# One 128-row load of the last V block, issued as three loads of 112, 8 and 8 rows

## The chip, the cores and the metric

The kernel runs on one core of one Trainium2 chip. The metric is device time in microseconds (us), as the median of several executions; besides these there is one profiled execution, from which every line of the profile comes. The core has a matrix engine (PE in the profile; PEld is its weight load), a vector engine (DVE), a scalar engine (ACT), GpSimd (POOL) and SyncE (SP), which in this kernel does nothing but issue transfers. The transfers themselves are carried out by the core's 16 DMA engines.

## The reference, cut to what matters

All arrays are float32. One token goes through four blocks: attention, MLP, attention, MLP, both attention blocks with the same caches and weights, and so both MLPs.

```python
def _A_ref(x, k_cache, v_cache, wq, wo):          # 32 heads, 4096 keys, 128 per head
    q = (x @ wq).reshape(B, Sq, H, Dh).transpose(0, 2, 1, 3)
    scores = jnp.einsum("bhqd,bhkd->bhqk", q, k_cache) * (Dh ** -0.5)
    p = _softmax(scores, axis=-1)
    o = jnp.einsum("bhqk,bhkd->bhqd", p, v_cache)
    return o.transpose(0, 2, 1, 3).reshape(B, Sq, H * Dh) @ wo

def _B_ref(x, w1, b1, w2, b2):                     # 512 -> 1376 -> 512
    return _gelu(x @ w1 + b1) @ w2 + b2

x = A_x
x = x + _A_ref(_layernorm(x), A_k_cache, A_v_cache, A_wq, A_wo)
x = x + _B_ref(_layernorm(x), B_w1, B_b1, B_w2, B_b2)
x = x + _A_ref(_layernorm(x), A_k_cache, A_v_cache, A_wq, A_wo)
x = x + _B_ref(_layernorm(x), B_w1, B_b1, B_w2, B_b2)
```

K and V hold 64 MB each and are needed in both layers, so that some 285 MB are read in all.

## The kernel before, in words

The 32 heads are worked in eight groups of four heads. K and V of a group are each one block of 128 rows (partitions) by 16384 columns, 8 MB. A block is cut into eight chunks of 2048 columns, numbered 0 to 7; a chunk is one step of the scores (K) or of the values (V) on PE. The first layer takes the groups upwards, the second downwards, so that what is still in SBUF at the change of layers is used again.

SBUF holds one large array, `arena`; every load goes to a place of it that is worked out by hand. All loads but one small one of vectors are issued by SP, through the helper `load` (L108 to L111 of the kernel before), each as one transfer of 128 rows, and they stay in the order in which the program calls `load`. A load waits until the place that it overwrites has been read. A load also signals its end on one of eight semaphores that the loads use in turn (DMAHW0 to DMAHW7 below), and it is not issued before the load that used the same semaphore last, eight loads earlier, has landed. So up to eight loads are issued and not yet landed, and the DMA engines work through them in the order of issue.

In a group, PE makes the scores from K, DVE and ACT make the exponentials, and the values are made partly by PE (`values`) and partly by DVE (`weighted`, `added`). The last group of the second layer is worked otherwise, from L579 on: its V block comes in four loads, which the table `LAST = ((0, 4), (4, 6), (6, 7), (7, 8))` gives as first and last chunk, and `values` multiplies each chunk on PE as soon as it has come. Behind these four loads SP issues the output weights of the group (one load of 2048 columns), the first MLP weights (2752, 1376 and 1376 columns) and the second MLP weights (2048, 2048, 1024 and 512 columns). These eight loads are the last of the program. `head_out`, `set_x` and `mlp` use them in that order, and the result, 2 KB, is written by SP at the end.

The generator `blocks` (L386) is what loads a block piece by piece and hands its chunks to the loop. The change touches `load`, `blocks` and the loop at L579.

Of the kernel before, what the change touches and what calls it, by code (L numbers as in the profile page):

```python
# [17 lines left out]
P = 128  # L18
# [5 lines left out]
C = 8  # L24
# [5 lines left out]
NC = 4 * U  # L30
# [24 lines left out]
W1_AT_END = ((0, 2), (2, 3), (3, 4))  # L55
LAST = ((0, 4), (4, 6), (6, 7), (7, 8))
W2_AT_CHANGE = (0, W1C, 2 * W1C, 3 * W1C, 10 * U, 11 * U)
W2_AT_END = (0, 4 * U, 8 * U, 10 * U, 11 * U)


@with_exitstack
def decode_layers(ctx: ExitStack, tc: tile.TileContext, vectors, k, v, w, w1, w2, out):
    nc = tc.nc
# [41 lines left out]
    def at(first, n):  # L105
        return arena[:, first : first + n]

    def load(first, src):  # L108
        t = at(first, src.shape[-1])
        tc.keep_in_program_order(nc.sync.dma_start(t, src))  # L110
        return t  # L111

    def matmul(*a, **kw):
# [5 lines left out]
    def quarters(first):  # L119
        return [at(first + U * j, U) for j in range(4)]  # L120

    def part(src, g, a, b):
        return src[g][:, NC * a : NC * b]

    def of_w(row, i, n):
        return w[row][:, NC * i : NC * (i + n)]

    def by_four(t):
        return t.rearrange("p (j n) -> p j n", j=4)


    wq_t = by_four(load(SHARED, of_w(1, 0, 1)))
    nc.vector.memset(wide, 1.0)
    nc.vector.memset(cells[:, WIDE:], 0.0)
# [52 lines left out]
    def set_x(xin0, scale, xin1, queries=True):  # L187
        s = small("x_sum")
        t = x_wide if queries else small("x1", 8)
        if not queries:  # L190
            nc.gpsimd.memset(pairs(t)[:, :, 1], 1.0)
        x = pairs(t)[:, :, 0]
        nc.vector.scalar_tensor_tensor(x, xin0, scale, xin1, op0=ALU.mult, op1=ALU.add, accum_out=s)
        if queries:
            for j in range(1, J):
                nc.gpsimd.tensor_copy(pairs(t[:, 32 * j :])[:, :, 0], x)
        return t, s

    def idle(to, n=U, of=C_AT, amid=False):
        matmul(to[:, :n], zero[:, 0:1].to_broadcast([P, P]), at(of, n), start=not amid, stop=not amid)  # L200
# [71 lines left out]
    def values(i, pt, vt, c):  # L272
        for j in range(J):
            matmul(pO[32 * j : 32 * j + 4, :], pt[:, c, j, :], vt[j],
                   start=(i == 0), stop=(i == C - 1))
# [11 lines left out]
    def added(home, by_pe=BY_PE):  # L287
        first, n = home + NC * by_pe, C - by_pe
        while n > 1:
            m = n // 2  # L290
            a, b = at(first + NC * (n - 2 * m), NC * m), at(first + NC * (n - m), NC * m)
            pinned(a, a, b, op=ALU.add)
            n -= m
        return quarters(first)
# [19 lines left out]
    def head_out(rl, wt, last=False, home=None, clear=0):  # L314
        on = head(rl, last)
        if clear:
            idle(pO[:, U - clear :], clear)
        to = pS if last else pO
        out_product(on, wt, to, last)
        return of_32(turned(to, not last, home), 4)  # L320
# [56 lines left out]
    def load_w1(first, a, b):  # L377
        load(first + W1C * a, w1[:, W1C * a : W1C * b])

    def load_w2(first, a, b):  # L380
        load(first + a, w2[:, a:b])

    def in_rows(first, n, rows):
        return [at(first + n * i, n) for i in range(rows)]

    def blocks(src, g, home, pieces=((0, C),)):  # L386
        for a, b in pieces:
            load(home + NC * a, part(src, g, a, b))
            for c in range(a, b):
                yield c, quarters(home + NC * c)  # L390

# [20 lines left out]
    def next_queries(xs, negm, wt, to=pO):  # L412
        for c in range(4):
            wide_query_block(to, c, xs, wt)
        z = queries(to, negm, wide=True)
        if to is pS:
            nc.vector.memset(pS, 0.0)
        return z
# [7 lines left out]
    def group(z, acc, ahead, k_blocks, out_behind=C - 2, change_banks=False):  # L426
        nonlocal pS, pO, pT, pM
        for c, t in k_blocks:
            scores(z, c, t)
            if ahead and c == SUM_BEHIND:  # L430
                t, rl, wt = ahead
                sum_up(t)
                on = head(rl)
            if ahead and c == out_behind:
                out_product(on, wt, pO)
        p = exponentials(sc, nsc)
        if ahead:
            acc = add_up(acc, of_32(turned(pO, wide=True), 4))
        if change_banks:
            pS, pO = pO, pS  # L440
            pT, pM = in_blocks(pO), pS
        return acc, *weights(p)

    def partly(pt, v_blocks, home, by_pe=BY_PE):
        for c, t in v_blocks:
            if c < by_pe:
                values(c, pt, t, c)
        weighted(pt, home, by_pe)
# [6 lines left out]
    for g in range(G):  # L455
        final = g == G - 1
        k_home, v_home = RING[2 * g % 3], RING[(2 * g + 1) % 3]
        acc, pt, rl = group(z, acc, ahead, blocks(k, g, k_home, HALVES if final else ((0, C),)))
        ahead = None
        if g == G - 2:  # L460
# [3 lines left out]
        if g < G - 2:  # L464
            partly(pt, blocks(v, g, v_home), v_home)
            pair = load(PAIR, of_w(g % 2, g, 2))
            z = next_queries(xs, negm, by_four(pair[:, NC:]), to=pS)
            ahead = added(v_home), rl, by_four(pair[:, :NC])
            continue
        for c, t in blocks(v, g, v_home, LAST if final else ((0, C),)):  # L470
            values(c, pt, t, c)
            if final and c in (5, 6):
                matmul(pO[:4, :], zero[:, 0:1].to_broadcast([P, 4]), at(C_AT, U), start=False, stop=False)
            if final and c == 7:
                idle_aside(3)
            if g == G - 2:
                for j in range(J):
                    i = 4 * c + j - KEPT_V // U
                    if i >= 0:
                        if pK[i] is pM:  # L480
                            nc.scalar.copy(tail, t[j][:, ASIDE:])
                            nc.scalar.copy(pM[:, :ASIDE], t[j][:, :ASIDE])
                        else:
                            nc.scalar.copy(pK[i], t[j])
# [21 lines left out]
    def behind_w2(c):  # L506
# [7 lines left out]
        if c == 9:  # L514
            begin_k(SHARED + 2 * NC, 2)

    own, xb = mlp(x1, s1, in_rows(SHARED, W1C, 4), in_rows(SHARED, U, FB),
                  lambda i: load_w2(SHARED, *W2_AT_CHANGE[i : i + 2]), behind_w2)
    xs, s = set_x(own, 1.0, xb)
    g = G - 2  # L520
# [30 lines left out]
    for i, first in enumerate([SHARED, SHARED + U] + [PAIR + U * j for j in range(4)]):  # L551
        t = at(first, U)
# [14 lines left out]
    for n in range(2, G):  # L567
        g, final = G - 1 - n, n == G - 1
        k_home, v_home = homes[(2 * n - 1) % 3], homes[2 * n % 3]
        acc, pt, rl = group(z, acc, ahead, blocks(k, g, k_home, HALVES if final else ((0, C),)),  # L570
                            C - 1 if final else C - 2, change_banks=final)
        if not final:
            by_pe = BY_PE_AT_BEGIN if n == 2 else BY_PE
            partly(pt, blocks(v, g, v_home, ((0, 6), (6, 8)) if n == 2 else ((0, C),)), v_home, by_pe)
            pair = load(PAIR, of_w(g % 2, g - 1, 2))
            z = next_queries(xs, negm, by_four(pair[:, :NC]), to=pS)
            ahead = added(v_home, by_pe), rl, by_four(pair[:, NC:])
            continue
        for c, t in blocks(v, g, v_home, LAST):  # L579
            values(c, pt, t, c)  # L580
            if c in (5, 7):
                idle(pS)
        wo_t = by_four(load(PAIR, of_w(g % 2, g, 1)))
        for a, b in W1_AT_END:
            load_w1(A_AT, a, b)
        for a, b in zip(W2_AT_END, W2_AT_END[1:]):
            load_w2(A_AT + 11 * U, a, b)
        own = head_out(rl, wo_t, last=True)
        idle(pO)
# [46 lines left out]
```

## Time and profile before

| | |
|---|---|
| median of 3 executions | 671.42 us (671.38 to 671.7) |
| profiled execution, its own time | 671.53 us |
| its span, first to last instruction | 669.8 us |
| mean granted TensorE clock | 0.804 |
| busy: PE, DVE, ACT | 57%, 56%, 4% of the span |
| DMA: mean rate, share of the last chain of work | 427 GB/s, 62% |
| HBM read | 285.35 MB |

The page of the profile gives the busy time of each engine, a strip of the span in 40 slices, the DMA queues (q1 is the queue of SP's loads), the chain of work that ended last, the costliest groups of instructions and the DMA issues. Views of the trace cut out stretches: busy time by windows, where the column before the last is the mean busy share of the 16 DMA engines and the last is what they moved in GB/s; the chain of waits in order of time; the instructions in order of time; and for the transfers of one tensor, the time from issue to landing. Times within the trace count from the span's start.

### The profile page before, as it was taken

To read this page: it belongs to the slowest core of one execution; us is meant where nothing else is said; L and a number is where in the kernel's file an instruction comes from. 1 tells how busy PE (TensorE), PEld (TensorE's weight loads), DVE (VectorE), ACT (ScalarE), POOL (GpSimd) and SP (SyncE) were. 2 spreads that over 40 slices of the span, in tenths; PEclk is the share of its full clock that TensorE was granted. 3 is DMA by queue.
4 is the path that set the end of the run, shared out by engine and by line. 5 is a ranking of instruction groups with operands and counts; after the bars stand their busy time and mean duration, and the time that the engine had idled before them with its cause. 6 is when DMAs were issued, how large, how long until landed. Compare 5 with 4: busy or idle time off the path is not lost.

```text
span 669.8 us, 5573 instructions
## 1 busy us (share of the span) xinstructions
PE 382.2 (57%) x2356; PEld 109.6 (16%) x2356; DVE 372.5 (56%) x474; ACT 29.7 (4%) x59; POOL 4.9 (1%) x23
## 2 busy tenths in 40 slices
PE   3441742636618446276778978627516456186686
PEld 1010110101101101011214222102101111021122
DVE  2049478395693965942212221492893966938831
ACT  0010000000000000002011120000000000000010
POOL 1000000000000000000000000000000000000000
PEclk9567875876778858787979999977859767786699
DMA  9999999999999999999999999999999999999996
GB/s 384 431 438 439 435 438 438 403 467 432 438 431 410 436 434 440 438 431 416 433 418 408 432 448 424 442 435 435 434 438 401 457 439 438 427 432 411 434 420 275
DMA packets 11544, 285.70 MB, mean 427 GB/s; under 512 B 1536, under 2 KB 1536, under 8 KB 3968
## 3 DMA queue, kind: packets, MB, share of 16 engines
q1 hardware_dynamic: 11376, 285.35, 99.0%
q8 instruction: 18, 0.29, 0.2%
q14 instruction: 6, 0.05, 0.0%
q10 hardware_dynamic: 144, 0.01, 0.0%
HBM read 285.35 MB, written 0.00 MB: 426 GB/s over the span
## 4 chain that ended last, share of the span: by engine, by line
DMA 62%; PE 28%; DVE 5%; another core or an unknown queue 2%; issue 1%; SPq 1%; ACT 0%; POOL 0%; DVEq 0%; ACTq 0%
DMA arena<-in_k 32%; DMA arena<-in_v 20%; PE pO L114 14%; PE pS L114 13%; DMA arena<-in_w 9%; DVE arena L280 3%; SPq L110 1%; DMA front<-in_vectors 1%; DVE arena L180 0%; ACT arena L117 0%; DVE arena L302 0%; PE pS L260 0%; DVE arena L184 0%; DVE cells L246 0%
## 5 line engine op out<-in xcount | busy, mean ns | idle before, releaser
L280 DVE TENSOR_TENSOR arena<-arena 128x2048 f32<-128x2048 f32 (+4 forms) x44 | 260.7, 5924 | 18.1 <-DMA arena<-in_v 17.3
L114 PE MATMUL pS<-arena,front 128*8 128x512 f32 (+2 forms) x466 | 72.6, 728 | 103.9 <-DMA arena<-in_k 103.9
L114 PE MATMUL pO<-arena,front 128*8 128x512 f32 (+3 forms) x602 | 86.1, 672 | 74.3 <-DMA arena<-in_k 49.0
L114 PE MATMUL pO<-arena,cells 128*128 128x512 f32 (+4 forms) x384 | 79.5, 462 | 21.6 <-DMA arena<-in_w 8.0
L114 PE MATMUL pS<-arena,cells 128*1 128x128 f32 (+3 forms) x320 | 58.4, 429 | 12.7 <-DMA arena<-in_w 9.7
L114 PE MATMUL pO<-arena 128*4 128x512 f32 x288 | 48.5, 806 | 19.9 <-DMA arena<-in_v 18.2
L302 DVE STREAM_TRANSPOSE arena<-pO 128x512 f32<-128x512 f32 x9 | 6.5, 717 | 63.6 <-PE pO L114 63.6
L114 PEld LDWEIGHTS pO<-arena,front 128*8 128x8 f32 (+1 forms) x602 | 19.3, 101 | 134.8 <-DVE arena L280 64.3
L114 PEld LDWEIGHTS pS<-arena,front 128*8 128x8 f32 (+1 forms) x466 | 15.0, 106 | 159.2 <-DVE arena L280 96.9
L180 DVE STREAM_TRANSPOSE arena<-pO 32x128 f32<-32x128 f32 x60 | 18.7, 312 | 39.3 <-PE pO L114 38.1
L114 PEld LDWEIGHTS pO<-arena,cells 128*128 128x128 f32 (+3 forms) x384 | 28.9, 122 | 69.9 <-issue 47.2
L114 PE MATMUL pS<-arena 128*4 128x512 f32 x216 | 32.2, 747 | 8.6 <-DMA arena<-in_v 7.4
L114 PEld LDWEIGHTS pS<-arena,cells 128*1 128x1 f32 (+3 forms) x320 | 23.1, 118 | 55.6 <-issue 42.9
L302 DVE STREAM_TRANSPOSE arena<-pS 128x512 f32<-128x512 f32 x7 | 5.0, 717 | 42.2 <-PE pS L114 42.2
L180 DVE STREAM_TRANSPOSE arena<-pS 32x128 f32<-32x128 f32 x48 | 15.0, 312 | 22.1 <-PE pS L114 21.0
L246 DVE TENSOR_REDUCE cells<-pO 128x1 f32<-128x512 f32 x9 | 6.2, 692 | 29.3 <-PE pO L114 29.2
L260 PE MATMUL pO<-front,arena 128*128 128x128 f32 x36 | 6.6, 313 | 25.1 <-ACT arena L117 25.1
L117 ACT ACTIVATE arena<-pO,cells 128x512 f32<-128x512 f32 x9 | 7.0, 779 | 268.8 <-DVE cells L251 268.8
L246 DVE TENSOR_REDUCE cells<-pS 128x1 f32<-128x512 f32 x7 | 4.8, 692 | 19.7 <-PE pS L114 19.5
L114 PEld LDWEIGHTS pO<-arena 128*4 128x4 f32 x288 | 7.8, 99 | 48.4 <-issue 40.4
L117 ACT ACTIVATE arena<-pS,cells 128x512 f32<-128x512 f32 x7 | 5.4, 778 | 231.8 <-DVE cells L251 231.8
L260 PE MATMUL pS<-front,arena 128*128 128x128 f32 x28 | 4.9, 304 | 18.6 <-ACT arena L117 18.6
(75 smaller groups left out, 105.0 us busy)
## 6 DMA issues: line engine op xcount, KB each, us to landing
arena<-in_w SPq DMA_DIRECT2D x13, 2048.0 KB, 11.7
arena<-in_k SPq DMA_DIRECT2D x4, 4096.0 KB, 25.2
arena<-in_v SPq DMA_DIRECT2D x2, 4096.0 KB, 39.7
arena<-in_w SPq DMA_DIRECT2D x9, 688.0 KB, 23.7
arena<-in_v SPq DMA_DIRECT2D x3, 2048.0 KB, 43.9
arena<-in_v SPq DMA_DIRECT2D x1, 6144.0 KB, 29.5
arena<-in_w SPq DMA_DIRECT2D x5, 1024.0 KB, 21.4
arena<-in_v SPq DMA_DIRECT2D x4, 1024.0 KB, 47.0
```

The source lines that it names most:

```text
L110: tc.keep_in_program_order(nc.sync.dma_start(t, src))
L114: tc.keep_in_program_order(nc.tensor.matmul(*a, **kw))
L117: tc.keep_in_program_order(nc.scalar.activation(*a, **kw))
L180: turn = nc.vector.transpose(t[q], src[q, P * j : P * (j + 1)])
L246: nc.vector.tensor_reduce(ml[:, 0:1], pS, axis=AX.X, op=ALU.max)
L260: tc.keep_in_program_order(nc.tensor.transpose(pT[:, b].rearrange("p j r -> p (j r)"), p[:, P * b : P * (b + 1)], ident))
L280: tc.keep_in_program_order(nc.vector.tensor_tensor(*a, **kw))
L302: nc.vector.transpose(ot, pO)
```

## The change

Chunks 4 and 5 of the last V block, 4096 columns or 16 KB of each row, were loaded as one transfer of 128 rows. Now rows 0 to 111 come as one transfer, rows 112 to 119 as a second, and rows 120 to 127 as a third, in this order. Source, destination and bytes are the same, and all other loads are as before.

```diff
 W2_AT_CHANGE = (0, W1C, 2 * W1C, 3 * W1C, 10 * U, 11 * U)
+UNEVEN = (0, 112, 120, 128)
 W2_AT_END = (0, 4 * U, 8 * U, 10 * U, 11 * U)
...
-    def load(first, src):
+    def load(first, src, rows=(0, P)):
         t = at(first, src.shape[-1])
-        tc.keep_in_program_order(nc.sync.dma_start(t, src))
+        for a, b in zip(rows, rows[1:]):
+            tc.keep_in_program_order(nc.sync.dma_start(t[a:b], src[a:b]))
         return t
...
-    def blocks(src, g, home, pieces=((0, C),)):
+    def blocks(src, g, home, pieces=((0, C),), uneven=()):
         for a, b in pieces:
-            load(home + NC * a, part(src, g, a, b))
+            load(home + NC * a, part(src, g, a, b), UNEVEN if a in uneven else (0, P))
             for c in range(a, b):
                 yield c, quarters(home + NC * c)
...
-        for c, t in blocks(v, g, v_home, LAST):
+        for c, t in blocks(v, g, v_home, LAST, uneven=(4,)):
             values(c, pt, t, c)
```

How this stands in SP's program, from the first load of the last V block to the last load but one; a row is the kernel's line, the operation, destination and source, rows by columns, and the semaphores waited for. (All weights are shown under one name, in_w.) Before:

```order
L110 DMA arena<-in_v 128x8192 [waits DMAHW6_49]
L110 DMA arena<-in_v 128x4096
L110 DMA arena<-in_v 128x2048
L110 DMA arena<-in_v 128x2048 [waits PE_49]
L110 DMA arena<-in_w 128x2048 [waits DMAHW7_49,DMAHW0_49,PE_49]
L110 DMA arena<-in_w 128x2752
L110 DMA arena<-in_w 128x1376 [waits DMAHW1_49,PE_49]
L110 DMA arena<-in_w 128x1376 [waits DMAHW2_49,PE_49]
L110 DMA arena<-in_w 128x2048 [waits DMAHW3_49,PE_49]
L110 DMA arena<-in_w 128x2048 [waits DMAHW4_49]
L110 DMA arena<-in_w 128x1024 [waits DMAHW5_49]
```

And now, on the same stretch of SP's program:

```order
L112 DMA arena<-in_v 128x8192 [waits DMAHW6_49]
L112 DMA arena<-in_v 112x4096
L112 DMA arena<-in_v 8x4096 x2
L112 DMA arena<-in_v 128x2048 [waits DMAHW7_49]
L112 DMA arena<-in_v 128x2048 [waits DMAHW0_49,PE_49]
L112 DMA arena<-in_w 128x2048 [waits DMAHW1_49,PE_49]
L112 DMA arena<-in_w 128x2752 [waits DMAHW2_49]
L112 DMA arena<-in_w 128x1376 [waits DMAHW3_49,PE_49]
L112 DMA arena<-in_w 128x1376 [waits DMAHW4_49,PE_49]
L112 DMA arena<-in_w 128x2048 [waits DMAHW5_49,PE_49]
L112 DMA arena<-in_w 128x2048 [waits DMAHW6_49]
L112 DMA arena<-in_w 128x1024 [waits DMAHW7_49]
```

One load became three, and since two more semaphores of the eight are taken up, each load behind them waits for a load that stands two places later in the queue than before.

On PE, the place is the values of the last group: its first two rows are chunks 0 to 3, then come chunks 4 and 5, then chunk 6. Before:

```order
L114 MATMUL pO<-arena 4x512 [waits DMAHW3_49,DVE_49]
L114 MATMUL pO<-arena 4x512 x15
L114 MATMUL pO<-arena 4x512 [waits DMAHW4_49]
L114 MATMUL pO<-arena 4x512 x7
L114 MATMUL pS<-arena,front 128x512
L114 MATMUL pO<-arena 4x512 [waits DMAHW5_49]
```

And now:

```order
L116 MATMUL pO<-arena 4x512 [waits DMAHW3_49,DVE_49]
L116 MATMUL pO<-arena 4x512 x15
L116 MATMUL pO<-arena 4x512 [waits DMAHW6_49,DMAHW5_49,DMAHW4_49]
L116 MATMUL pO<-arena 4x512 x7
L116 MATMUL pS<-arena,front 128x512
L116 MATMUL pO<-arena 4x512 [waits DMAHW7_49]
```

The matmuls and their order are the same; the first matmul of chunk 4 waits for three loads in place of one.

## The prediction

> **What bounds the kernel now.** I read the chain of waits first, over the last 80 us, since the change sits there. Columns: start, length, what.
>
> ```profile
> 601.39 0.43 SPq L110
> 601.83 0.04 issue
> 601.87 46.19 DMA arena<-in_v
> 648.05 0.02 issue
> 648.07 17.79 DMA arena<-in_w
> 665.86 0.04 issue
> 665.90 1.05 PE pS L114 x24
> 666.96 0.02 issue
> 666.98 0.33 DVE arena L184
> 667.31 0.02 issue
> 667.33 0.16 DVE cells L593
> ```
>
> From 601.87 to 665.86 the chain is transfers alone; behind them stand 1.05 + 0.33 + 0.16 us of work and the write of the result. So whatever moves the landing of the last weights moves the end one for one. The busy time by windows shows how full the DMA engines are (second number from the right: their busy share; last: GB/s):
>
> ```profile
> 450.00:500.00 50.00, 23.06 (x112) 5.97 (x116) 34.28 (x32) 0.87 (x2) 0.00 (x0) 0.74 1.01 435
> 600.00:655.00 55.00, 38.43 (x222) 10.13 (x214) 36.06 (x50) 3.23 (x6) 0.31 (x2) 0.81 0.99 426
> ```
>
> All 16 are busy, at 435 GB/s, which is 27.2 GB/s each. A row of 4096 columns is 16384 bytes, so one engine needs 16384 / 27.2e3 = 0.60 us for it. The queue of SP's loads tells how rows are shared out:
>
> ```profile
> q1 hardware_dynamic: 11376, 285.35, 99.0%
> ```
>
> SP issues 79 transfers of 128 rows, the result's among them; 11376 / 79 = 144 = 128 + 16. I read this as one packet per row and one closing packet per engine: every transfer before is spread over all 16 engines, 8 rows each.
>
> Then the end of the stream, in half microseconds:
>
> ```profile
> 662.00:662.50 0.50, 0.17 (x8) 0.19 (x12) 0.00 (x0) 0.00 (x0) 0.00 (x0) 1.00 0.99 410
> 662.50:663.00 0.50, 0.50 (x27) 0.48 (x22) 0.00 (x0) 0.00 (x0) 0.00 (x0) 1.00 0.78 315
> 663.00:663.50 0.50, 0.50 (x17) 0.28 (x6) 0.00 (x0) 0.00 (x0) 0.00 (x0) 1.00 0.73 299
> 663.50:664.00 0.50, 0.50 (x2) 0.11 (x2) 0.00 (x0) 0.00 (x0) 0.00 (x0) 1.00 0.60 242
> 664.00:664.50 0.50, 0.44 (x2) 0.00 (x0) 0.00 (x0) 0.00 (x0) 0.00 (x0) 1.00 0.51 197
> 664.50:665.00 0.50, 0.31 (x12) 0.30 (x16) 0.00 (x0) 0.00 (x0) 0.00 (x0) 1.00 0.25 98
> 665.00:665.50 0.50, 0.50 (x28) 0.43 (x18) 0.00 (x0) 0.00 (x0) 0.00 (x0) 1.00 0.12 49
> 665.50:666.00 0.50, 0.34 (x16) 0.10 (x8) 0.00 (x0) 0.00 (x0) 0.00 (x0) 1.00 0.12 45
> 666.00:666.50 0.50, 0.50 (x16) 0.21 (x10) 0.00 (x0) 0.00 (x0) 0.00 (x0) 1.00 0.01 4
> ```
>
> The engines do not end together although each had the same bytes. At 663 about 12 of 16 are at work, at 664.25 about 8, at 664.75 about 4, and from 665 to 666 two (0.12 is 2/16). The first end near 662.5, the last at 666.0: **the end is set by the two engines that are latest, some 1.2 us behind the other fourteen.** They don't wait for one another, since all loads are queued long before, so a delay of one engine is carried to the end.
>
> **The change part by part.** *Bytes per engine.* 112 rows spread over 16 engines are 7 each. A transfer of 8 rows can use at most eight engines, with a row each. If both small transfers use the same eight, these carry 7 + 1 + 1 = 9 rows and the other eight carry 7. Against 8 before that is +0.60 us on eight engines and −0.60 us on the other eight. The trace does not name engines, so which eight the late ones belong to is open: −0.60 at the end if both are among the relieved, +0.60 if one is not. [...]
>
> *The way into the rows.* Before, the 16 engines write to different parts of the 128 rows, eight rows each, and the rate is an even 435 GB/s. Now eight engines write at once into eight neighbouring rows. No row of the trace has anything like that. Bounds: below, nothing, if the 27.2 GB/s is the engine's own limit. Above, if eight neighbouring rows are served by one path of 27.2 GB/s, the eight rows go one after another, 8 x 0.60 = 4.8 us instead of 0.60, or +4.2 us for each small transfer, +8.4 for both. The nearest row is the 435 GB/s itself: it is reached with every engine in rows of its own, and 27.2 GB/s per eight rows is all that has been seen to enter them. That favours a limit; but how eight rows share paths is unknown, and I take the middle, two paths and four rows deep: 4 x 0.60 = 2.4 us, +1.8 us per transfer, +3.6 for both. With the extra row that is +4.2 us for the eight engines if they arrive in step. They do not: they are spread over 3.5 us (662.5 to 666.0), more than the 2.4 us that such a transfer lasts, so that half the queueing, +1.8, may be met: 0.6 + 1.8 = +2.4. If neither of the two latest is among the eight, 1.2 us of this is free, as the others end that much earlier: +3.0 in step, +1.2 out of step. The mean of 4.2, 2.4, 3.0 and 1.2 is **+2.7 us**, with +1.2 to +5 as the range of this case (5 for other engines whose own rows lie behind the same paths).
>
> [...]
>
> *SP and its queue.* Two more issues, of the size of these (time order, start and length):
>
> ```profile
> 600.93 1.84 SPq L110 DMA_DIRECT2D arena<-in_v  x4
> 616.62 34.20 SPq L110 DMA_DIRECT2D arena<-in_w  x8
> 667.52 0.35 SPq L594 DMA_DIRECT2D out<-cells  x1
> ```
>
> 1.84 / 4 = 0.46 us each, 0.9 us in all, on an engine that is waiting anyway. The moved waits matter more: each load behind the small ones now waits for the load eight issues earlier, which stands two places later. The landings, of the four V loads and of the two K loads ahead of them, counted from issue (minimum/median/maximum):
>
> ```profile
> L110 SPq DMA_DIRECT2D arena<-in_v x4: 422/430/432, 600.9 to 602.3; - x4
> DMA to landing us min/median/max: 39.8/45.2/48.1
> L110 SPq DMA_DIRECT2D arena<-in_k x2: 384/404/424, 600.0 to 600.5; - x2
> DMA to landing us min/median/max: 20.3/24.9/29.5
> ```
>
> K lands at 620.3 and 630.0, V's first piece at 640.8, chunks 4 and 5 at about 645.6 (640.8 and 4096 x 4 x 128 bytes at 435 GB/s, 4.8 us), its last at 602.3 + 48.1 = 650.4. The output weights were issued at 616.62 and now wait for 620.3; the first 1376-column load waits for 640.8 instead of 620.3, the second for 645.6 instead of 630.0. At 645.6 there are still queued 2048 + 2048 + 2048 + 2752 + 1376 columns, 10272 x 4 x 128 bytes = 5.3 MB, 12 us at 435 GB/s. The queue never runs dry: cost nothing. Without this cover it would be what a load into a short queue takes from issue to landing, about 5.6 us:
>
> ```profile
> arena<-in_w SPq DMA_DIRECT2D x1, 496.0 KB, 5.6
> ```
>
> The last load waits for the last V piece as it did.
>
> *PE.* It waits for three loads at chunk 4 instead of one:
>
> ```profile
> 643.24 5.33 PE L114 MATMUL pO<-arena 128*4 128x512 f32 x48 [1.68 <-DVE arena L263]
> 649.56 2.01 PE L114 MATMUL pO<-arena 128*4 128x512 f32 x16
> 653.05 1.05 PE L114 MATMUL pS<-arena,cells 128*1 128x128 f32 x32 [0.42 <-DMA arena<-in_w]
> 665.90 1.01 PE L114 MATMUL pS<-arena,cells 128*1 128x128 f32 x24 [0.16 <-DMA arena<-in_w]
> ```
>
> Chunks 0 to 5 take 5.33 us from 643.24, and what follows waits for weights again and again. Chunks 4 and 5 some 3 us late push their own 16 matmuls (a third of 5.33, 1.8 us), and the loads behind are late by as much: nothing is added.
>
> Sum: 0 + 0 + 2.7 us on the profiled execution's 671.53 (span 669.8 and 1.7 around it) is 674.2; on the median of 671.42, 0.1 us lower, **674.1 us**, 0.4% slower.
>
> **The rivals.** *No queueing, late engines relieved* (chance 0.22): 671.42 − 0.60 = 670.8. For it: the steady 27.2 GB/s per engine looks like an engine's own limit. It cannot give more, as one row is all that is moved. *No queueing, a late engine among the eight* (0.16): 672.0. *The 112 rows lose their spread too* (0.09): with seven rows per engine the shares no longer stand apart as with eight. Four engines on one path throughout would make 7 rows 16.9 us instead of 4.2, +12.6; half of that, as they fall out of step, +6: 677.4. Against it: shares of seven neighbouring rows still cover 112 different rows. *SP falls short of loads* (0.02), if landing signals come in late by more than the 12 us: +5.6, 677.0. *Faster by more than a row explains* (0.05): the two latest engines are late through something that falls elsewhere now, −1.8 at most, since fourteen are done at about 664.8 and the relieved ones another 0.6 earlier: 669.6.
>
> **How the numbers follow.** Queueing as summed has 0.46, and 674.1 is its time; its own range is 672.6 to 676.4. From 670.6 to 677.5 about eight in ten are held: left out are the faster rival, most of the 112-row case and the slow end of the first. A difference of 0.2%, 1.34 us, is about what a measurement of this kernel can tell from no change. Within it: 0.22 + 0.16 and the mildest 0.05 of queueing, 0.43. Slower: 0.41 + 0.09 + 0.02 = 0.52. Faster: 0.05.
>
> **What would show it.** Packets of q1: 78 x 144 + (112 + 16) + 2 x (8 + 8) = 11392 if the small transfers use eight engines each, 11408 if all 16 post their end. With queueing, a window of about 5 us near 641 to 650 falls below 426 GB/s and the last-engine steps end near 669; without it the rate stays and only the steps move, by 0.6 us. Wrong I would be if the GB/s stays at its level there, or if the drop lasts as long as the 112 rows take. A wait of SP with an empty queue, seen as a share far below 1 between 650 and 660, would show the SP rival.

## The result

The changed kernel takes 678.81 us (median of 4 runs, 678.45 to 679.12) against 671.44 us before (4 runs, 671.38 to 671.7): a ratio of 1.0108, 95% interval 1.0096 to 1.012, so **7.4 us slower**. The forecast was 674.1, with a range up to 677.5. The span of the profiled execution went from 669.8 to 677.3 us.

### The profile after, beside that of before

The chain of waits of the changed kernel over its last 80 us (start, length, what):

```profile
605.96 49.62 DMA arena<-in_v
...
655.60 17.55 DMA arena<-in_w
673.19 0.62 PE pS L116 x16
673.81 0.44 PE pS L116 x8
674.27 0.33 DVE arena L186
674.62 0.16 DVE cells L595
```

It is the same chain: V, then the last weights, then 1.6 us of work. The transfers of V end at 655.58, where before they ended at 648.06, and the weights take as long as before (17.55 us against 17.79). All of the loss lies ahead of the weights.

The busy time by windows of the changed kernel (window, its length, busy time of the engines, granted clock, and as the last two the busy share of the DMA engines and GB/s):

```profile
638.00:640.00 2.00, 2.00 (x5) 0.95 (x6) 1.52 (x5) 0.20 (x1) 0.00 (x0) 1.00 0.88 197
640.00:642.00 2.00, 2.00 (x8) 0.88 (x6) 0.56 (x3) 1.97 (x4) 0.10 (x1) 1.00 1.01 229
642.00:644.00 2.00, 0.32 (x5) 0.11 (x8) 1.86 (x9) 0.18 (x1) 0.00 (x0) 1.00 1.07 238
644.00:646.00 2.00, 2.00 (x24) 0.54 (x20) 0.00 (x0) 0.00 (x0) 0.00 (x0) 1.00 0.88 184
646.00:648.00 2.00, 1.33 (x16) 0.11 (x4) 0.00 (x0) 0.00 (x0) 0.00 (x0) 1.00 1.33 213
648.00:650.00 2.00, 0.00 (x0) 0.00 (x0) 0.00 (x0) 0.00 (x0) 0.00 (x0) 1.00 0.82 111
650.00:652.00 2.00, 0.00 (x0) 0.00 (x0) 0.00 (x0) 0.00 (x0) 0.00 (x0) 0.51 0.85 172
652.00:654.00 2.00, 0.50 (x4) 0.14 (x8) 0.00 (x0) 0.00 (x0) 0.00 (x0) 0.50 0.92 332
654.00:656.00 2.00, 2.00 (x12) 0.30 (x8) 0.00 (x0) 0.00 (x0) 0.00 (x0) 0.50 1.01 426
```

From 638 to 652 the DMA engines look as busy as ever, and move about half as much or less: 184 to 238 GB/s and then 111 and 172, where 435 had been steady. At 654 the rate is back. One row for the whole stretch, first of the changed kernel:

```profile
638.00:654.00 16.00, 8.15 (x48) 2.73 (x52) 3.94 (x16) 2.35 (x4) 0.10 (x1) 0.88 0.97 209
```

and the same window of the kernel before:

```profile
638.00:654.00 16.00, 13.90 (x112) 4.36 (x110) 4.63 (x19) 2.36 (x4) 0.10 (x1) 1.00 0.98 417
```

(417 − 209) GB/s over 16 us are 3.3 MB that did not come, and 3.3 MB at 435 GB/s are 7.7 us: the whole of the loss is in this stretch. The busy share tells nothing of it (0.97 against 0.98), so share and rate have to be read side by side.

The trace also keeps each packet of a transfer with its size, start and duration, though not its engine; in these loads a packet is one row. Before, each of the 128 rows of chunks 4 and 5 (16 KB) took 0.61 us. Now all but three of them took longer, 1.18 us in the median: the rows of the 112-row load are slow themselves, and not only the 16 others. They come between 637.0 and 652.5 us, where before they came between 636.8 and 645.2. As a mean over the 16 engines, these rows cost 5.2 us more than before, and rows of whole loads that came at the same time (1.2 MB took over a tenth longer than usual) cost another 2.8 us.

PE, in order of time in the changed kernel, with the idle time before each group and what ended it:

```profile
643.72 3.62 PE L116 MATMUL pO<-arena 128*4 128x512 f32 x32 [1.68 <-DVE arena L265]
653.50 3.54 PE L116 MATMUL pO<-arena 128*4 128x512 f32 x16 [6.17 <-DMA arena<-in_v]
```

Chunks 0 to 3 are multiplied at 643.72, and then PE stands still until the three loads of chunks 4 and 5 have landed, at 653.5, where before the chunks 0 to 5 were one run of matmuls from 643.24 to 648.57. PE is a follower here: it waits, and the weights behind the V block are late by themselves.

The queue of SP's loads:

```profile
q1 hardware_dynamic: 11392, 285.35, 99.1%
```

11392 packets are 78 x (128 + 16) + (112 + 16) + 2 x (8 + 8): read as one closing packet per engine, as the prediction reads them, an eight-row load closes on eight engines only.

### The profile page after: what moved, and what is told of

It is laid out like the page before. It is cut to its first block, busy times and chain, and to the rows that moved or that the text cites. A ratio compares the mean times of both kernels' runs of the same rounds, so it can differ in the third digit from the quotient of the medians.

```text
span 677.3 us, 5577 instructions
## 1 busy us (share of the span) xinstructions
PE 390.3 (58%) x2356; PEld 111.3 (16%) x2356; DVE 372.3 (55%) x474; ACT 29.6 (4%) x59; POOL 4.8 (1%) x23
## 3 DMA queue, kind: packets, MB, share of 16 engines
q1 hardware_dynamic: 11392, 285.35, 99.1%
## 4 chain that ended last, share of the span: by engine, by line
DMA 66%; PE 25%; DVE 5%; another core or an unknown queue 2%; issue 1%; SPq 0%; ACT 0%; POOL 0%; DVEq 0%; ACTq 0%
DMA arena<-in_v 29%; DMA arena<-in_k 23%; DMA arena<-in_w 14%; PE pO L116 13%; PE pS L116 12%; DVE arena L282 3%; DMA front<-in_vectors 1%; SPq L112 0%; DVE arena L182 0%; ACT arena L119 0%; DVE arena L186 0%; DVE arena L304 0%; DVE cells L248 0%; DVE pO L419 0%
## 5 line engine op out<-in xcount | busy, mean ns | idle before, releaser
L116 PE MATMUL pO<-arena,front 128*8 128x512 f32 (+3 forms) x602 | 88.6, 690 | 71.5 <-DMA arena<-in_k 45.9
L116 PE MATMUL pO<-arena,cells 128*128 128x512 f32 (+4 forms) x384 | 81.4, 467 | 20.3 <-DMA arena<-in_w 6.9
L116 PE MATMUL pS<-arena,cells 128*1 128x128 f32 (+3 forms) x320 | 61.0, 438 | 13.8 <-DMA arena<-in_w 10.4
L116 PE MATMUL pS<-arena 128*4 128x512 f32 x216 | 35.0, 803 | 8.8 <-DMA arena<-in_v 7.6
```

Source lines behind the costliest of these rows:

```text
L116: tc.keep_in_program_order(nc.tensor.matmul(*a, **kw))
```

## The experiments

Each kernel was timed beside the kernel before on the same chip (medians of 671.46 to 671.51 us there). Theory 1, *paths*, supposes that a load of fewer than 128 rows gives the engines rows that lie behind shared paths into SBUF. Theory 2, *pieces*: each added load costs by being issued, signalled and waited for. Theory 3 is the prediction's: only the eight-row loads queue. Theory 4 came later: the rows as they lie in HBM are what is slow. The edits are shown cut to what matters.

### Is it the number of loads?

`e1_columns`: three loads again, but cut by columns.

```diff
-        for a, b in zip(rows, rows[1:]):
-            tc.keep_in_program_order(nc.sync.dma_start(t[a:b], src[a:b]))
+        cols = (0, 3584, 3840, 4096) if rows is UNEVEN else (0, src.shape[-1])
+        for a, b in zip(cols, cols[1:]):
+            tc.keep_in_program_order(nc.sync.dma_start(t[:, a:b], src[:, a:b]))
```

> The load of chunks 4 and 5 is cut in three by columns (3584, 256 and 256 columns of all 128 rows), so that the number of loads and the semaphore waits behind them are those of the change, and no load has fewer than 128 rows. Theory 1 (paths: a transfer of fewer than 128 rows gives the engines shares of rows that lie behind the same paths into SBUF, so that they get in each other's way, in the 112-row load too): no difference, 671.4 us, within 0.5. Theory 2 (pieces: each added load costs by being issued, signalled and waited for): the whole loss, 678.8. Theory 3 (the prediction: only eight engines writing into eight neighbouring rows queue): no difference, 671.4.

Measured: 671.82 us against 671.48, ratio 1.0005, interval 0.9995 to 1.0014. No difference is shown; the 0.3 us between the medians are within the interval. Its windows over the V block and behind it:

```profile
640.00:650.00 10.00, 7.75 (x62) 1.73 (x60) 2.19 (x10) 0.52 (x2) 0.10 (x1) 1.00 1.00 419
650.00:660.00 10.00, 7.40 (x80) 2.52 (x80) 2.27 (x12) 0.00 (x0) 0.75 (x2) 1.00 1.01 426
```

The rate stays at 419 to 426 GB/s. With the same number of loads and the same semaphore waits, nothing of the loss is left that could be told. Theory 2 is out.

### Is it the eight-row loads alone?

`e2_112_16` keeps the 112 rows and joins the two small loads to one of 16 rows; `e3_64_64` has two halves.

```diff
-UNEVEN = (0, 112, 120, 128)
+UNEVEN = (0, 112, 128)      # e2_112_16
+UNEVEN = (0, 64, 128)       # e3_64_64
```

> The 112-row load stays, the other 16 rows come as one load, a row for each engine, so no engine has more bytes than another. Theory 1: in the changed kernel DMA moves 215 GB/s at a busy share of 0.98 while the 112 rows come, half of 435, so 7 rows take 8.4 us instead of 4.2, +4.2; 16 neighbouring rows at four paths, four deep, +1.8; together about 677.4, with the same low GB/s for 8 us. Theory 2: one added load of two, half the loss, 675.1. Theory 3: the 16-row load alone, +1.8, 673.2, with 430 GB/s while the 112 rows come.

> The load is cut into rows 0 to 63 and 64 to 127: four rows for each engine in each, no load of eight rows. Theory 1: 64 neighbouring rows reach half of the paths, two engines to each, so both loads run at about 215 GB/s, 9.6 us instead of 4.8: +4.8, 676.2. Theory 2: one added load of two, 675.1, with no stretch of half rate. Theory 3: no load of eight rows, so no difference, 671.4.

Measured: 679.11 us (ratio 1.0112, interval 1.0097 to 1.0127) and 679.03 us (1.0113, 1.0096 to 1.013). Theory 1 had expected 677.4 and 676.2. Both lose as much as the change, without any eight-row load. In `e2_112_16` the rate halves while the 112 rows come:

```profile
640.00:642.00 2.00, 2.00 (x6) 0.81 (x5) 0.78 (x4) 1.25 (x3) 0.00 (x0) 1.00 1.03 229
642.00:644.00 2.00, 0.98 (x6) 0.45 (x4) 1.35 (x6) 1.10 (x2) 0.10 (x1) 1.00 1.18 254
```

and in `e3_64_64` over the whole of

```profile
638.00:652.00 14.00, 8.06 (x42) 2.34 (x40) 2.79 (x13) 2.36 (x4) 0.10 (x1) 0.88 0.95 218
652.00:660.00 8.00, 6.66 (x35) 1.48 (x36) 0.16 (x1) 0.00 (x0) 0.00 (x0) 0.79 1.01 423
```

Theory 3 is out as a whole account. Theory 1 has the half rate right (218 GB/s in `e3_64_64`, where 215 was expected), and its size too small: 676.2 was expected there, 679.0 came. At half rate the 2.1 MB of the two loads would take 9.6 us; the slow stretch lasts 14 us, and 218 GB/s over 14 us are 3.05 MB. So nearly 1 MB of the loads beside them was slowed with them. The packets agree: here the rows of the two halves cost 4.7 us more per engine, and 1.0 MB in rows of whole loads another 2.0.

### Does the loss go by bytes?

```diff
-        for c, t in blocks(v, g, v_home, LAST, uneven=(4,)):
+        for c, t in blocks(v, g, v_home, LAST, uneven=(6,)):
```

> Chunks 4 and 5 come whole; chunk 6, of half the bytes, is cut into 112, 8 and 8 rows in their place. Theory 1: the loss goes by bytes, half of 7.4: +3.7, 675.1. Theory 2: the loss goes by the number of loads: +7.4, 678.8. Theory 3: half of what the eight-row loads cost, +1.4, 672.8.

Measured: 677.33 us, ratio 1.0087, interval 1.0072 to 1.0102: +5.9 us with half the bytes, between the two expectations. Of the 7.4 us, 1.5 go with the halved bytes; so most of the loss does not shrink with them. Since the number of loads costs nothing (`e1_columns`), I read the rest as the time until the last of the engines, which are some 3.5 us apart, has left the rows in question. The rate bears this out in part: it stayed at 213 to 238 GB/s from 642 to 652 us, 10 us for half the bytes against 14 to 16 us for all of them. That it is the engines' distance is argued, not shown.

### What do such loads cost by themselves?

All V loads whole, and one or two more loads between the MLP weights, into columns that nothing reads.

```diff
+        for rows in (slice(0, 128),):                        # x1_all
+        for rows in (slice(0, 112),):                        # x2_112
+        for rows in (slice(112, 120), slice(120, 128)):      # x3_8_near
+        for rows in (slice(0, 32, 4), slice(1, 32, 4)):      # x4_8_apart
+            spare = at(A_AT + 22 * U, 2 * NC)[rows]
+            tc.keep_in_program_order(nc.sync.dma_start(spare, part(v, g, 4, 6)[rows]))
         for a, b in zip(W2_AT_END, W2_AT_END[1:]):
```

> All loads are as before the change; one more load is put between the first and second MLP weights: chunks 4 and 5 of the same V block once more, 128 rows of 4096 columns, into columns that nothing reads. It measures what such a load costs by itself. All theories: 2 MB at 435 GB/s, +4.8 us, 676.2.

> As the kernel before with one more load of rows 0 to 111 of 4096 columns into columns that nothing reads. Theory 1 (paths): seven rows for each engine at half rate, 8.4 us: +8.4, 679.8, and about 215 GB/s while they come. Theory 3 (only eight-row loads queue): 7 x 0.60, +4.2, 675.6. That this load with fewer bytes costs more than the one of 128 rows is what only theory 1 says.

> As the kernel before with two more loads of eight rows of 4096 columns, rows 112 to 119 and 120 to 127, into columns that nothing reads. Theories 1 and 3: the eight engines of such a load queue, four to a path: 2 x 2.4 = 4.8 us on these engines if they arrive in step, half of the queueing if not, 1.2 us of it free if the latest engines are not among the eight: +1.8 to +4.8, 673.2 to 676.2. Without any queueing: two rows, +1.2 at most, 672.6.

> As the run with two more loads of eight neighbouring rows, but the eight rows of each stand four rows apart (0, 4, ... 28 and 1, 5, ... 29), so that by theory 1 each engine has a path of its own. Theory 1: no queueing, two rows more on eight engines: +1.2 us if one of the latest engines is among the eight, 0 if none is: 671.4 to 672.6, at least 1 us less than with neighbouring rows. If rows don't matter and what costs is a transfer that uses eight engines only, the same time as with neighbouring rows.

Measured: 677.72, 683.38, 675.61 and 678.26 us, against 671.47 before; that is +6.3, +11.9, +4.1 and +6.8. The first is 1.5 us more than its bytes explain. Its DMA does not account for that: the rate stays up, as in the first line below. PE does, whose work from there on is the rest of the chain: it waited 5.59 us for the weights behind the added load, its granted clock was 0.50 from 666 to 672, and the 32 matmuls that ran next took 1.89 us, where the kernel before took 1.05. In `x2_112` they took the same 1.89. The lines are two of `x1_all`'s windows, then these matmuls before, in `x1_all` and in `x2_112`:

```profile
664.00:666.00 2.00, 0.00 (x0) 0.00 (x0) 0.00 (x0) 0.00 (x0) 0.00 (x0) 0.88 1.02 430
666.00:672.00 6.00, 4.58 (x50) 2.07 (x54) 0.00 (x0) 0.00 (x0) 0.00 (x0) 0.50 0.55 224
662.33 1.05 PE L114 MATMUL pS<-arena,cells 128*1 128x128 f32 x32 [0.97 <-DMA arena<-in_w]
667.42 1.89 PE L116 MATMUL pS<-arena,cells 128*1 128x128 f32 x32 [5.59 <-DMA arena<-in_w]
673.01 1.89 PE L116 MATMUL pS<-arena,cells 128*1 128x128 f32 x32 [7.18 <-DMA arena<-in_w]
```

So the two can be compared: these matmuls start 5.59 us later in `x2_112` than in `x1_all`, by the transfers alone. **The load of 112 rows costs 5.7 us more than the load of 128 rows** of the same columns, with an eighth fewer bytes. Of theories 1 to 3 only the first says that (it had expected 8.4 against 4.8, a difference of 3.6 us), and it is the part that the prediction had put at nothing. Its windows:

```profile
660.00:662.00 2.00, 0.00 (x0) 0.00 (x0) 0.00 (x0) 0.00 (x0) 0.00 (x0) 0.67 0.91 205
662.00:664.00 2.00, 1.50 (x9) 0.35 (x10) 0.11 (x1) 0.00 (x0) 0.00 (x0) 0.50 1.04 209
664.00:666.00 2.00, 1.83 (x2) 0.25 (x2) 0.91 (x3) 0.21 (x1) 0.00 (x0) 0.50 0.97 221
666.00:668.00 2.00, 0.00 (x0) 0.00 (x0) 0.00 (x0) 0.00 (x0) 0.00 (x0) 0.50 0.95 217
```

`x4_8_apart` looks like a refutation of theory 1, and is not one. Its DMA windows, first those of `x3_8_near`, then its own:

```profile
656.00:658.00 2.00, 1.55 (x19) 0.54 (x18) 0.41 (x4) 0.00 (x0) 0.00 (x0) 1.00 1.15 228
658.00:660.00 2.00, 0.61 (x10) 0.35 (x10) 0.25 (x4) 0.00 (x0) 0.55 (x1) 1.00 0.96 218
660.00:662.00 2.00, 0.70 (x8) 0.05 (x8) 0.00 (x0) 0.00 (x0) 0.00 (x0) 0.93 1.03 216
```

```profile
656.00:658.00 2.00, 0.00 (x0) 0.00 (x0) 0.00 (x0) 0.00 (x0) 0.00 (x0) 0.79 1.03 431
658.00:660.00 2.00, 0.00 (x0) 0.00 (x0) 0.00 (x0) 0.00 (x0) 0.00 (x0) 0.50 1.02 432
660.00:662.00 2.00, 1.26 (x28) 0.86 (x32) 0.41 (x2) 0.00 (x0) 0.00 (x0) 0.50 1.00 422
```

The rate stays at 422 to 432 GB/s where the neighbouring rows had 216 to 228. The time was lost elsewhere, by a wait that stepped rows brought into the program (who waited for the added loads, in `x4_8_apart`):

```profile
  DVE cells L308: 7.2, 1
```

DVE waited 7.2 us for two loads that it does not read (I take it that the program's dependences treat rows in steps as if they overlapped other columns; no run shows it), and PE, whose columns in the windows above are empty until 660, waited for DVE. So this run's time says nothing on theory 1, and its rate does (422 to 432 GB/s); by the packets each of the 16 added rows took 0.61 us and no row beside them was slowed.

### Written rows or read rows?

The two eight-row loads right behind chunks 4 and 5, which come whole; read and written rows chosen apart (`pairs` stands for the rows in the last four lines).

```diff
+        if rows is UNEVEN:                    # behind the whole load
+            spare = at(A_AT + 22 * U, 2 * NC)
+            for to, of in pairs:
+                tc.keep_in_program_order(nc.sync.dma_start(spare[to], src[of]))
+        # y1_near        to 112..119, 120..127               of 112..119, 120..127
+        # y2_to_apart    to 0, 4, ... 28 and 1, 5, ... 29     of 112..119, 120..127
+        # y3_from_apart  to 112..119, 120..127               of 0, 4, ... 28 and 1, 5, ... 29
+        # y4_apart64     to 64, 68, ... 92 and 65, ... 93     of 112..119, 120..127
```

> Chunks 4 and 5 come as before the change, in one load of 128 rows; right behind it come two more loads of eight neighbouring rows (112 to 119, 120 to 127) of the same columns, into columns that nothing reads. It is the eight-row part of the change by itself and in its place. By theory 1 (paths into SBUF) and by theory 4 (rows that lie together in HBM are slow to read by eight engines at once) the loss is that measured between the MLP weights, +4.1: 675.6, with GB/s near 220 for some 6 us. By a theory of the place (the loss comes from something that waits there) it differs by over 1 us.

> The same two loads, read from the same neighbouring rows of HBM, but written to rows 0, 4, ... 28 and 1, 5, ... 29 of SBUF. Theory 1: the eight engines of a load write to rows of eight different paths, in each case those of their own usual rows, and nothing queues: 420 GB/s or more throughout, 671.4 to 672.7. Theory 4: as with neighbouring rows, 675.6.

> The other half: read from rows 0, 4, ... 28 and 1, 5, ... 29 of HBM, written to the neighbouring rows 112 to 119 and 120 to 127 of SBUF. Theory 1: 675.6, GB/s near 220 for some 6 us. Theory 4: 671.4 to 672.7.

> The same two loads, read from neighbouring rows, written to rows 64, 68, ... 92 and 65, 69, ... 93. Theory 1 in its strict form, a path belongs to a group of rows and not to an engine: the eight engines have eight paths, but those that the other eight engines are using for their own rows, two engines to a path. Each of these paths has two rows more to take, so the other eight engines, if the latest are among them, end up to 2 x 0.6 = 1.2 us later: 672.6, and GB/s falls by about a quarter for some 3 us. If it is enough that the eight engines keep apart from each other: as with rows 0 to 29, 671.4, without a drop of GB/s.

Measured: 675.37 (ratio 1.0059, interval 1.0044 to 1.0074), 676.69 (1.0076, 1.0061 to 1.0091), 675.16 (1.0057, 1.0042 to 1.0072) and 676.05 us (1.0067, 1.005 to 1.0085), against 671.46. `y1_near` is as expected, and the place is not what matters. `y3_from_apart` settles theory 4: read from rows apart, written to neighbouring rows, it loses the same, and its rate falls to

```profile
644.00:646.00 2.00, 2.00 (x24) 0.53 (x20) 0.00 (x0) 0.00 (x0) 0.00 (x0) 1.00 0.98 180
646.00:648.00 2.00, 0.75 (x8) 0.00 (x0) 0.00 (x0) 0.00 (x0) 0.00 (x0) 1.00 0.85 188
```

The two runs with stepped written rows were inconclusive. Their loads were not issued before 644.3 us, again by a wait that stepped rows brought, and the queue ran empty. In `y2_to_apart`:

```profile
644.00:646.00 2.00, 1.70 (x16) 0.43 (x20) 0.53 (x3) 0.00 (x0) 0.00 (x0) 1.00 0.28 82
```

A share of 0.28 is a dry queue, not a slow one.

### The same with a full queue

The added loads were moved behind the last V load, where 644 us is early enough (`uneven=(7,)` in the code above).

```diff
+            spare, again = at(A_AT + 22 * U, 2 * NC), part(v, 0, 4, 6)
+            for to, of in pairs:              # all of 112..119, 120..127
+                tc.keep_in_program_order(nc.sync.dma_start(spare[to], again[of]))
+        # z1_near to 112..119, 120..127; z2_to_apart to 0, 4, ... 28 and 1, 5, ... 29;
+        # z3_to_apart64 to 64, 68, ... 92 and 65, 69, ... 93
```

> The V block comes whole, in four loads of 128 rows, and behind the last of them come two more loads of eight rows of 4096 columns, read from neighbouring rows and written to neighbouring rows 112 to 119 and 120 to 127 of columns that nothing reads. It is the measure for the two runs beside it. Theory 1: +3.9, 675.4, as behind chunks 4 and 5, with a stretch of some 6 us near 210 GB/s.

> The same reads at the same place in the queue, written to rows 0, 4, ... 28 and 1, 5, ... 29; this place is chosen so that the queue does not run empty, as it did behind chunks 4 and 5, where the share fell to 0.28. Theory 1: each engine writes among its own usual rows, nothing queues, GB/s stays above 400, and the end moves by 0 to 1.2 us (two rows more on eight engines): 671.4 to 672.7. If stepped rows don't help: 675.4, as with neighbouring rows.

> The same reads at the same place, written to rows 64, 68, ... 92 and 65, 69, ... 93. Theory 1, strict (a path belongs to rows): the eight engines share paths with the other eight, two to each; GB/s falls to about 330 for 2 to 3 us and the end moves by up to 1.2 us, 672.7 if the latest engines are among those whose rows these are. If it only matters that the eight engines stay apart from each other: GB/s above 400 as with rows 0 to 29.

Measured: 675.03 us (ratio 1.0054, interval 1.0039 to 1.0069), 671.81 us (1.0004, 0.9995 to 1.0014) and 674.25 us (1.0041, 1.0026 to 1.0056), against 671.51. The windows of the three in this order:

```profile
648.00:650.00 2.00, 2.00 (x21) 0.33 (x13) 0.00 (x0) 0.00 (x0) 0.00 (x0) 1.00 1.05 188
650.00:652.00 2.00, 2.00 (x14) 0.40 (x10) 0.00 (x0) 0.00 (x0) 0.00 (x0) 1.00 0.94 190
652.00:654.00 2.00, 0.11 (x8) 0.02 (x7) 0.00 (x0) 0.00 (x0) 0.00 (x0) 1.00 0.93 236
```

```profile
648.00:650.00 2.00, 2.00 (x14) 0.41 (x10) 0.00 (x0) 0.00 (x0) 0.00 (x0) 1.00 1.01 427
650.00:652.00 2.00, 1.79 (x14) 0.41 (x10) 0.45 (x1) 0.00 (x0) 0.00 (x0) 1.00 1.03 439
652.00:654.00 2.00, 1.41 (x34) 0.76 (x32) 0.68 (x3) 0.00 (x0) 0.00 (x0) 1.00 0.98 414
```

```profile
648.00:650.00 2.00, 1.75 (x10) 0.11 (x8) 0.00 (x0) 0.00 (x0) 0.00 (x0) 1.00 0.99 225
650.00:652.00 2.00, 0.00 (x0) 0.00 (x0) 0.00 (x0) 0.00 (x0) 0.00 (x0) 1.00 0.98 224
652.00:654.00 2.00, 0.87 (x8) 0.11 (x8) 0.00 (x0) 0.00 (x0) 0.00 (x0) 0.93 0.99 374
```

The edits differ only in the rows that are written to. The stepped rows again brought a wait, so that their two loads were issued later; first `z1_near`, then the two others:

```profile
627.78 0.66 SPq L115 DMA_DIRECT2D arena<-in_v  x2
642.85 1.46 SPq L115 DMA_DIRECT2D arena<-in_v  x2
642.09 1.47 SPq L115 DMA_DIRECT2D arena<-in_v  x2
```

It did no harm here, as no share in the windows falls below 0.93, and `z2_to_apart` and `z3_to_apart64` are alike in it. Neighbouring rows: 188 to 236 GB/s and +3.5 us. Rows four apart in the first quarter: 414 to 439 GB/s and no difference that can be told. Rows four apart in the third quarter: 225 GB/s for 4 us and +2.7 us, though the rows are spaced as in the run before; theory 1 had expected about 330 GB/s there. The packets say the same: in `z2_to_apart` each of the 16 added rows took 0.61 us and no row beside them was slowed, in `z3_to_apart64` 14 of the 16 took longer, 1.11 us in the median of the 16, and with them 1.1 MB in rows of whole loads. So for eight-row loads the written rows decide; that is shown. Theory 1 in its strict form, by which a path belongs to rows, fits this and is not shown: the traces don't name engines, so no run says which of them would meet in `z3_to_apart64`. Nor is it shown that the loads of 112 and 64 rows are slow for the same reason: written and read rows were parted for eight-row loads only. What theory 1 had too small is again the size, 1.2 us for the end of `z3_to_apart64` where 2.7 came.

## Why the prediction was wrong

The forecast of slower was right, its size not: +2.7 us predicted, +7.4 measured, outside the range. Point by point:

- **What bounds the kernel.** Right. The chain is the same, and what moved the stream moved the end.
- **The step that failed: the sum "0 + 0 + 2.7 us", which has no term for the 112-row load.** In it the 112 rows cost what their bytes cost, and their losing the spread was a rival with a chance of 0.09 and 677.4 us (half of its 12.6 would be 677.7), which is where the kernel went and past it. By itself a load of 112 rows costs 5.7 us more than one of 128 (`x2_112` and `x1_all`), and with 112 + 16 rows the loss is that of the change (`e2_112_16`, +7.6). What was said against the rival, that seven neighbouring rows to an engine still cover 112 different rows, misses the point: the rows are different, and 109 or more of them were slow in the changed kernel all the same. The argument that led to a limit of 27.2 GB/s per group of rows for the small loads held for the large one as well, and was not applied to it. What the runs show in its place: rows of 16 KB that take 1.18 us in the median instead of 0.61, and whole loads beside them that are slowed too.
- **The eight-row loads, +2.7.** By themselves +3.5 (`z1_near`) and +3.9 (`y1_near`, `x3_8_near` +4.1): inside the case's own range of +1.2 to +5, and the term was too small by about 1 us. That it came so near is partly luck. No run shows the two paths, four rows deep, which I took as a middle between two bounds: by that estimate a row would have taken up to 2.4 us, and in `z1_near` the 16 rows took 1.30 us in the median; most of that loss is in rows of whole loads beside them (2.6 us per engine, against 0.6), for which the sum had no term (only the upper end of the range allowed for them). In the changed kernel the parts do not add: 112 rows with 16 and with 8 + 8 lose the same 7.4 to 7.6 us.
- **Bytes per engine, −0.60 or +0.60.** That both small loads use the same eight engines was assumed, and no run shows it; the packets show eight closing packets for each. The two eight-row loads without queueing moved the end by 0.3 us (`z2_to_apart`, interval of the ratio 0.9995 to 1.0014, up to 0.9 us), where 1.2 was possible. So the eight engines that a small load uses seem not to be the latest ones, and the −0.60 may have been there; no run shows it, and in the change it was covered by twelve times its worth.
- **SP, its queue and the moved waits, 0.** Right: `e1_columns` has the same waits and no loss.
- **PE waiting for three loads, 0.** Right as to the end: PE waited 6.17 us at chunk 4, its 16 matmuls took 3.54 us at a granted clock of 0.50 where 1.8 was reckoned with, and the weights behind were late by themselves.
- **What would show it.** The packet count of 11392 came out as given. The drop was expected for about 5 us; it lasted some 15 to 16, and a drop as long as the 112 rows take was named as the sign of being wrong.

**What stays open** is why the written rows matter, and part of the size. The traces show the rate, 435 GB/s for loads of 128 rows and 218 in `e3_64_64`, and not which engine writes which row. If two engines on a path simply halve each other, as theory 1 had it, the halves cost `e3_64_64` 4.8 us and it lost 7.5; `z3_to_apart64` should have lost 1.2 and lost 2.7. The packets say where most of the surplus is: in `e3_64_64` the rows of the halves did cost 4.7 us per engine, and rows of whole loads beside them 2.0 more; in `z3_to_apart64` the added rows cost 0.4 and those beside them 1.9, and the slow rows lie between 647.2 and 653.5 us, about as long as the added rows come (646.6 to 652.4). That whole loads are slowed until the latest engine has left the rows of the cut load would fit this and `e4_chunk6`, where half the bytes kept four fifths of the loss (5.9 of 7.4 us). It is not shown: no run was made that brings the engines into step, and no trace says how the sum of such delays falls on the engine that ends last. No run points to a version faster than the kernel before: the lowest medians, 671.81 us (`z2_to_apart`) and 671.82 (`e1_columns`), are not below its 671.51 and 671.48. Other ways of giving rows to engines were not tried.

## What to carry to other kernels

A load that is cut by rows can cost far more than its bytes: here every cut of the 128 rows of chunks 4 and 5 (112 + 8 + 8, 112 + 16, 64 + 64) halved the rate of the DMA engines together for 14 us or more (192, 195 and 218 GB/s in the mean from 638 to 652 us, where 435 had been steady), while the same load cut by columns into three pieces kept 419 to 426 GB/s and cost nothing that could be told (671.82 us against 671.48). If a load like this one is to be split, split its columns and keep 128 rows; if few rows must be loaded beside a full stream, the rows they were written to decided here, and equal spacing was not enough (414 to 439 GB/s in `z2_to_apart` against 225 in `z3_to_apart64`). And a busy share near 1.0 does not mean full rate, as it was 0.97 at 209 GB/s and 0.98 at 417: compare the GB/s of the stretch with that of a quiet one.

## What the hardware showed that I had not expected

- A load of eight rows is slow or not by which rows it writes to: 188 to 236 GB/s into neighbouring rows, 414 to 439 into rows four apart from row 0 on, and 225 into rows four apart from row 64 on (`z1_near`, `z2_to_apart`, `z3_to_apart64`).
- Loads that were whole and merely stood beside the cut ones were slowed too: in `e3_64_64` 3.05 MB came at half rate (218 GB/s), and the cut loads hold 2.1 MB.
- The loss hardly depends on how the rows are cut (7.4, 7.6 and 7.5 us for the three cuts) and only weakly on the bytes (5.9 us for half of them).
